# Reordering the last stage of an attention and two-layer MLP kernel: earlier operand taking, later square, separate PSUM pools

## The chip, the cores and the metric

The kernel runs on one core of a Trainium2 chip. The metric is the device time of one execution in microseconds (us), lower is better. A profiled execution gives the span of the core's instructions and the trace.

## The reference

```python
def reference(q, k, v, w1, w2, w3, w4, g_ln):      # names shortened
    x = causal_softmax_attention(q, k, v)          # 2 x 12 heads, 448 x 64, fp32
    x = x.transpose(0, 2, 1, 3).reshape(896, 768)
    h = x @ w1; x = (h * sigmoid(h)) @ w2          # 768 -> 2048 -> 768
    h = x @ w3                                     # 768 -> 1024
    e = exp(h - max(h)); s = h * e / (sum(e) + 1e-9)
    ln = (s - mean(s)) / sqrt(var(s) + 1e-6) * g_ln
    return ln @ w4                                 # 1024 -> 768
```

## The kernel before

All matrix products of the MLPs are made with operands split into a high and a low part (`fp32r`), three matmuls for each block of 128 x 128: high by high, high by low, low by high. Attention and the first MLP come first; the change touches only what follows, the second MLP.

There the 896 tokens are seven tiles of 128 (tile 0 to 6). `gemm3(t)` makes the 1024 columns of `h` of a tile in two PSUM banks. `chain(t)` makes the softmax-weighted value and its normalisation from them: VectorE (DVE) takes the negated maximum, ScalarE (ACT) the exponential, DVE the product `e * h / sum`, ACT the square with the mean as bias (written over `h` in PSUM, summed to the variance) and the shift by the mean (Identity, in place), then DVE and GpSimd (POOL) make the factor `rstd[t]`.

The last product needs `e` transposed. `turn(t)` does that on TensorE (PE), 16 small transposes into a two-bank PSUM tile `tp`. `take(t, n)` brings half n of it to SBUF: ACT copies the high part (L694), DVE makes the low part by a subtraction (L695). Tiles 0, 1 and 2 go through `whole(t, n)`: for each half n of the output two "products" of twelve matmuls each, into one of two PSUM banks (`gm`), then an ACT copy scaled by `rstd` (L739) and a store. Tiles 3 and 4, and then 5 and 6, go through `pair4`, a Strassen-like scheme with seven products for each pair, which needs sums of operand halves (made in `pre`, additions L701 on DVE, splits on ACT and POOL) and sums of weight quarters (`sums4`: four ACT scalings L833 and four POOL subtractions L835 to L838; `split_t`: four ACT copies L843 and four DVE subtractions L844). `pair4` takes its banks in turn from `psq` and `gm`.

There are 12 products in `whole` and 14 in `pair4`. After each of them `after()` runs the next entry of the table `steps`, in which the preparing work is put by hand; entry n runs behind product number n, counted from 0. Each engine works through its instructions in the order in which the program issues them. Two engines that read the same PSUM bank take turns in program order: the tile library adds a wait between them. `turn` uses the pools in the list `turns` in rotation: `pst`, and `pstb` after it has been appended. Before the change `pst` alone serves tiles 0 and 1, and `pstb` and `psq` take over the four banks of `psh`, in which `gemm3` wrote, once `chain(6)` is through.

Of the kernel before, what the change touches and what calls it, by code (L numbers as in the profile page):

```python
# [8 lines left out]
F32 = mybir.dt.float32  # L9
F32R = mybir.dt.float32r  # L10
U32 = mybir.dt.uint32
AF = mybir.ActivationFunctionType
ALU = mybir.AluOpType
# [13 lines left out]
K2 = KF2 // 2  # L27
NT = T // 128
# [52 lines left out]
def fused(ctx, tc, qk, vv, w1, w2, w3, w4, gl, out):  # L81
    nc = tc.nc
    PS = bass.MemoryType.PSUM

    def pool(name, bufs=1, **kw):
        return tc.alloc_tile_pool(name=name, bufs=bufs, **kw)
# [29 lines left out]
    with tc.manual_schedule():  # L116
# [338 lines left out]
        for step in ORDER.split():  # L455
            step, _, n = step.partition("/")
            e = {"A": nc.scalar, "V": nc.vector, "G": nc.gpsimd}.get(step[-1])
            step, _, part = step.rstrip("AVG").partition(".")
            name = step.rstrip("0123456789")
# [19 lines left out]
        for f in range(KF):  # L479
            if f == 1:  # L480
                gps[f, 1] = gm.tile([128, 512], F32, name="ps", tag="gm")
            else:
                t = pair()
# [3 lines left out]
            for half in range(2):  # L487
# [3 lines left out]
                m = 2 * f + half + 4  # L491
# [89 lines left out]
        dp = pool("dp", 1)  # L581
        pad(dp, 256)
        aop = {}
# [46 lines left out]
        hps, rstd, es4 = {}, {}, {}  # L630
        psd.release()
        pst = pool("pst", 1, space=PS)
        psh = pool("psh", 2, space=PS)

        def columns(t):
            n, b = divmod(t - 1, B)
# [1 line left out]
            return slice(o, o + 128)  # L638

        def gemm3(t):  # L640
            ps = psh.tile([128, 2, 512], F32, name="h", tag="h")
            at = columns(t)
            for n in range(2):
                for k in range(KD):
                    o = (n * KD + k) * 512
                    wh, wl = woven(w3h[:, o:o + 512]), woven(w3l[:, o:o + 512])
                    nc.tensor.matmul(ps[:, n], yh[:, k, at], wh, start=k == 0, stop=False)  # L647
                    nc.tensor.matmul(ps[:, n], yh[:, k, at], wl, start=False, stop=False)  # L648
                    nc.tensor.matmul(ps[:, n], yl[:, k, at], wh, start=False, stop=k == KD - 1)  # L649
            hps[t] = ps  # L650

        def half(t, n):
            return es4[t][:, K2 * n:K2 * n + K2]

        def chain(t, fill, fill2):
            ps = hps[t]
            s = dp.tile([128, 12], F32, name="s", tag="s", bufs=NT)
            es4[t] = dp.tile([128, KF2, 128], F32, name="e", tag="e", bufs=NT - 1)
            e, p3 = es4[t], ps.rearrange("p n (m q) -> p (n m) q", m=K2)
            col = lambda m: s[:, m:m + 1]  # L660
            nc.vector.tensor_reduce(col(0), ps, AX.XY, ALU.max, negate=True)
            nc.scalar.activation(e, p3, AF.Exp, bias=col(0), accum_out=col(1))
            fill()
            nc.vector.tensor_scalar(col(2), col(1), 1e-9, None, ALU.add)
            nc.vector.reciprocal(col(3), col(2))
            nc.vector.scalar_tensor_tensor(e, e, col(3), p3, ALU.mult, ALU.mult, accum_out=col(4))
            nc.vector.tensor_scalar(col(5), col(4), -1.0 / DF2, None, ALU.mult)
            fill2()
            nc.scalar.activation(p3, e, AF.Square, bias=col(5), accum_out=col(6))
            nc.scalar.activation(e, e, AF.Identity, bias=col(5))  # L670
            nc.vector.tensor_scalar(col(7), col(6), 1.0 / DF2, 1e-6, ALU.mult, ALU.add)
            nc.gpsimd.tensor_tensor(col(9), col(7), mhalf, ALU.pow)
            rstd[t] = col(9)

        tps = {}
# [3 lines left out]
        def rows(a):  # L679
            return a.rearrange("p k (z q) -> p k z q", q=C)  # L680

        def turn(t):
            turns.append(turns.pop(0))
            tp = turns[-1].tile([128, 2, 512], F32, name="tp", tag="tp")
            for m in range(KF2):
                for z in range(2):
                    r = slice(C * z, C * z + C)
                    nc.tensor.transpose(tp[:, z, C * m:C * m + C], es4[t][r, m], ident[r, r])
            both = tp.rearrange("p z (m q) -> p m z q", q=C)
            tps[t, 1], tps[t, 2] = both[:, :K2], both[:, K2:]  # L690

        def parts(z, x, low):
            h, l = [rows(a) for a in aop[z]]
            nc.scalar.activation(h, x, AF.Copy)  # L694
            low.tensor_tensor(l, x, h.bitcast(F32), ALU.subtract)  # L695

        def take(t, n, z=None):
            parts(z or (t, n), tps[t, n], nc.vector)

        def add(o, a, b, op):  # L700
            nc.vector.tensor_tensor(o, a, b, op)  # L701

        banks = [gm, gm]
# [28 lines left out]
        def whole(t, n):  # L732
            if n == 0:
                outs[t] = four()
            o, ps = outs[t][n], bank()
            for k in (1, 2):
                product(ps, (t, k), f"{k}{n + 1}", k == 1, k == 2)
                if k == 2:
                    nc.scalar.activation(o, ps, AF.Copy, scale=rstd[t])  # L739
                    store(t, n, o)  # L740
                after()
# [51 lines left out]
        for t in range(NT):  # L793
            gemm3(t)
            if t == 0:
                fill()
            if t == NT - 2:
                turn(0)

            def first():  # L800
                if t == NT - 2:
                    take(0, 1)
                    take(0, 2)
                fill()

            if t < NT - 1:
                chain(t, first, fill)
        area = act.tile([128, 2 * KD * T], F32R, name="area", tag="a")[:, 8:]
        places = {(1, 1): 0, (1, 2): 1, (2, 1): 2, (2, 2): 3}
        for g, at in ((1, (4, 5, 6, 7, 8, 9, None)), (2, (0, 1, 2, 3, None, 4, 5))):  # L810
# [6 lines left out]

        def arrive(t):
            turn(t)
            take(t, 1)  # L820
            take(t, 2)

        while pend:
            fill()
        w3p.release()
# [5 lines left out]
        def sums4(k):  # L831
            for n, z in enumerate(QUADS):
                nc.scalar.activation(quads[z, k], quads[z, k], AF.Copy, scale=gain[:, k + K2 * (n // 2):k + K2 * (n // 2) + 1])  # L833
            b11, b12, b21, b22 = [quads[z, k] for z in QUADS]
            nc.gpsimd.tensor_tensor(b11, b12, b11, ALU.subtract)  # L835
            nc.gpsimd.tensor_tensor(b12, b12, b22, ALU.subtract)
            nc.gpsimd.tensor_tensor(b22, b22, b11, ALU.subtract)
            nc.gpsimd.tensor_tensor(b21, b21, b22, ALU.subtract)  # L838

        def split_t(k):  # L840
            for z, q in (("t2", "22"), ("t3", "12"), ("t1", "11"), ("t4", "21")):
                h, l = split[4, z]
                nc.scalar.activation(h[:, k], quads[q, k], AF.Copy)  # L843
                nc.vector.tensor_tensor(l[:, k], quads[q, k], h[:, k].bitcast(F32), ALU.subtract)  # L844

        def pre(g, n):
            a, b = 2 * g + 1, 2 * g + 2
            s1, s3, s2, s4 = [rows(half(*at)) for at in ((b, 1), (b, 0), (a, 0), (a, 1))]
            if n == 0:
                turn(b)  # L850
                nc.scalar.activation(s3, tps[b, 1], AF.Copy)
                add(s1, tps[b, 2], s3, ALU.add)
                take(b, 2, (g, "22"))
            elif n == 1:
                turn(a)
                take(a, 1, (g, "11"))
                add(s2, s1, tps[a, 1], ALU.subtract)
                add(s3, s3, tps[a, 1], ALU.subtract)
            elif n == 2:
                take(a, 2, (g, "12"))  # L860
                add(s4, tps[a, 2], s2, ALU.subtract)
                parts((g, "s4"), s4, nc.gpsimd)
            else:
                z = ("s2", "s3", "s1")[n - 3]
                parts((g, z), {"s1": s1, "s2": s2, "s3": s3}[z], nc.gpsimd)

        steps = {1: [lambda: sums4(1)], 2: [lambda: split_t(0)], 3: [lambda: arrive(2)], 4: [lambda: sums4(2)],
                 5: [lambda: pre(1, 0)], 6: [lambda: sums4(3)], 7: [lambda: pre(1, 1)], 8: [lambda: split_t(1)],
                 9: [lambda: pre(1, 2)], 10: [lambda: split_t(2)], 11: [lambda: split_t(3), lambda: pre(1, 3)],
                 12: [lambda: pre(1, 4)], 13: [lambda: pre(1, 5)],  # L870
                 14: [lambda: pre(2, 0)], 15: [lambda: pre(2, 1)], 16: [lambda: pre(2, 2)],
                 17: [lambda: pre(2, 3), lambda: pre(2, 4)], 18: [lambda: pre(2, 5)]}
        at = iter(range(26))
# [2 lines left out]
            for step in steps.get(next(at), ()):  # L876
                step()

        def takes():
            take(1, 1)  # L880
            take(1, 2)

        sums4(0)
        turn(1)
        chain(NT - 1, takes, lambda: whole(0, 0))
        psh.release()
        psq = pool("psq", 2, space=PS)
        turns.append(pool("pstb", 1, space=PS))
        whole(0, 1)
        for t in (1, 2):  # L890
            for n in range(2):
                whole(t, n)
        banks[0] = psq
        for g in (1, 2):
            pair4(g)
        turns.remove(pst)
# [57 lines left out]
```

## Time and profile before

| | us |
|---|---|
| time, median of 3 runs | 408.81 |
| lowest and highest of them | 407.88, 411.54 |
| the profiled execution | 408.6 |
| its span | 406.8 |
| PE busy, share of the span | 396.9, 98% |
| DVE, ACT, POOL busy | 346.9, 239.7, 204.5 |

The profiled execution lies 0.2 us under the median of the runs, and its time is 1.8 us longer than its span. In the rows below a timeline line gives the start in us, the duration in us, the engine, the line of the kernel, the operation and the tiles written and read; square brackets give the idle time of the engine just before it and what ended it.

### The profile page before, as it was taken

To read this page: it belongs to the slowest core of one execution; us is meant where nothing else is said; L and a number is where in the kernel's file an instruction comes from. 1 tells how busy PE (TensorE), PEld (TensorE's weight loads), DVE (VectorE), ACT (ScalarE), POOL (GpSimd) and SP (SyncE) were. 2 spreads that over 40 slices of the span, in tenths; PEclk is the share of its full clock that TensorE was granted. 3 is DMA by queue.
4 is the path that set the end of the run, shared out by engine and by line. 5 is a ranking of instruction groups with operands and counts; after the bars stand their busy time and mean duration, and the time that the engine had idled before them with its cause. 6 is when DMAs were issued, how large, how long until landed. Compare 5 with 4: busy or idle time off the path is not lost.

```text
span 406.8 us, 7567 instructions
## 1 busy us (share of the span) xinstructions
PE 396.9 (98%) x2649; PEld 368.0 (90%) x2649; DVE 346.9 (85%) x739; ACT 239.7 (59%) x551; POOL 204.5 (50%) x222
## 2 busy tenths in 40 slices
PE   7999999999999999999999999999999999999896
PEld 5777778899999999999999999999988888889796
DVE  4999999899999999997998979867999997546843
ACT  5999999444535353534644445444658775987630
POOL 2997863377777777776453434333400010665440
PEclk9999999999999999999999999999999999999999
DMA  7775412133525242424766757555033310011121
GB/s 254 255 273 169 138 45 79 40 117 117 153 82 148 85 151 83 147 88 139 243 197 172 230 176 214 182 158 155 2 93 103 116 39 2 19 41 39 40 79 60
DMA packets 19799, 50.05 MB, mean 123 GB/s; under 512 B 2352, under 2 KB 4528, under 8 KB 19760
## 3 DMA queue, kind: packets, MB, share of 16 engines
q1 hardware_dynamic: 19760, 49.56, 39.4%
q8 instruction: 21, 0.34, 0.3%
q14 instruction: 18, 0.15, 0.1%
HBM read 46.80 MB, written 2.75 MB: 122 GB/s over the span
## 4 chain that ended last, share of the span: by engine, by line
PE 82%; DVE 8%; ACT 6%; DMA 2%; POOL 0%; SPq 0%; issue 0%; DVEq 0%
PE h L381 8%; PE h L380 8%; PE h L382 8%; PE h L510 7%; PE h L509 7%; PE h L508 7%; PE x L258 5%; PE h L647 4%; PE h L649 4%; PE h L648 4%; PE x L232 3%; DVE e L198 2%; PE x L168 2%; PE ps L715 2%; PE ps L713 2%; PE ps L714 2%
## 5 line engine op out<-in xcount | busy, mean ns | idle before, releaser
L316 POOL TENSOR_TENSOR wl<-wx,wh 128x384 fp32r<-128x384 f32 x64 | 80.6, 1261 | 73.6 <-ACT wh L312 49.0
L285 ACT ACTIVATE wr<-wr 128x384 f32<-128x384 f32 x96 | 56.7, 593 | 34.1 <-DMA wr<-w_in 34.0
L296 DVE SCALAR_TENSOR_TENSOR wx<-wr,wx 128x384 uint32<-128x384 uint32 x96 | 70.0, 730 | 0.1
L312 ACT ACTIVATE wh<-wx 128x384 fp32r<-128x384 f32 x64 | 33.1, 519 | 58.1 <-DVE wx L296 32.8
L306 DVE TENSOR_SCALAR wr<-wr 128x384 uint32<-128x384 uint32 x96 | 59.0, 614 | 3.5 <-DMA wr<-w_in 3.2
L290 DVE SCALAR_TENSOR_TENSOR wx<-wr 128x384 uint32<-128x384 uint32 x96 | 60.6, 632 | 1.3 <-POOL gl L391 1.3
L382 PE MATMUL h<-x,wl 128*128 128x448 f32 x174 | 61.3, 352 | 0.0
L380 PE MATMUL h<-x,wh 128*128 128x448 f32 x174 | 61.3, 352 | 0.0
L381 PE MATMUL h<-x,wh 128*128 128x448 f32 x174 | 61.3, 352 | 0.0
L509 PE MATMUL h<-gl,wh 128*128 128x448 f32 x160 | 56.4, 352 | 0.0
L510 PE MATMUL h<-gh,wl 128*128 128x448 f32 x160 | 56.4, 352 | 0.0
L508 PE MATMUL h<-gh,wh 128*128 128x448 f32 x160 | 56.4, 352 | 0.0
L218 POOL TENSOR_TENSOR e<-e,st 128x128 f32<-128x128 f32 (+3 forms) x70 | 44.0, 664 | 19.5 <-DVE st L211 14.7
L391 POOL TENSOR_TENSOR gl<-sg,gh 128x448 fp32r<-128x448 f32 x32 | 40.5, 1267 | 16.6 <-DVE gh L390 9.6
L204 ACT ACTIVATE e<-e,st 128x128 f32<-128x128 f32 (+3 forms) x84 | 43.6, 527 | 3.5 <-DVE st L198 3.4
L198 DVE CUSTOM_DVE_ANT_0 e<-x,mask 128x128 f32<-128x128 f32 (+3 forms) x84 | 33.1, 445 | 4.7 <-PE x L168 4.6
L382 PEld LDWEIGHTS h<-x,wl 128*128 128x128 f32 x174 | 32.9, 189 | 0.1
L381 PEld LDWEIGHTS h<-x,wh 128*128 128x128 f32 x174 | 32.9, 189 | 0.0
L380 PEld LDWEIGHTS h<-x,wh 128*128 128x128 f32 x174 | 32.9, 189 | 0.0
L647 PE MATMUL h<-w3h,y 128*128 128x512 f32 x84 | 31.9, 380 | 0.0
L648 PE MATMUL h<-w3l,y 128*128 128x512 f32 x84 | 31.8, 379 | 0.0
L649 PE MATMUL h<-w3h,y 128*128 128x512 f32 x84 | 31.8, 379 | 0.0
(204 smaller groups left out, 864.9 us busy)
## 6 DMA issues: line engine op xcount, KB each, us to landing
wr<-w_in SPq DMA_DIRECT2D x96, 384.0 KB, 3.6
qk<-qk_in SPq DMA_DIRECT2D x11, 480.0 KB, 5.4
v<-vv_in SPq DMA_DIRECT2D x12, 256.0 KB, 5.2
out<-o SPq DMA_DIRECT2D x12, 192.0 KB, 1.9
out<-o SPq DMA_DIRECT2D x4, 96.0 KB, 2.2
qk<-qk_in SPq DMA_DIRECT2D x2, 128.0 KB, 2.4
qk<-qk_in SPq DMA_DIRECT2D x1, 224.0 KB, 2.7
gain<-gl_in SPq DMA_DIRECT2D x1, 4.0 KB, 3.5
```

Of the source, the lines that this page charges most:

```text
L285: nc.scalar.activation(high, high, AF.Copy, scale=DOWN)
L290: nc.vector.scalar_tensor_tensor(x.bitcast(U32), r[:, :, 1], 0x80000000, r[:, :, 0], ALU.bitwise_and, ALU.bitwise_or)
L296: nc.vector.scalar_tensor_tensor(xu, r[:, :, 1], 3, xu, ALU.logical_shift_left, ALU.bitwise_or)
L306: nc.vector.tensor_scalar(low, low, 29, None, ALU.logical_shift_right)
L316: eng.tensor_tensor(l, wx.pop((n, c)), h.bitcast(F32), ALU.subtract)
L380: nc.tensor.matmul(ps[:, :S], wh, rh, start=turn == 0 and k % NB == 0, stop=False)
L381: nc.tensor.matmul(ps[:, :S], wh, rl, start=False, stop=False)
L382: nc.tensor.matmul(ps[:, :S], wl, rh, start=False, stop=turn == 1 and k % NB == NB - 1)
L508: nc.tensor.matmul(ps[:, :S], wh, rh, start=f == 0, stop=False)
L509: nc.tensor.matmul(ps[:, :S], wh, rl, start=False, stop=False)
L510: nc.tensor.matmul(ps[:, :S], wl, rh, start=False, stop=f == KF - 1)
L647: nc.tensor.matmul(ps[:, n], yh[:, k, at], wh, start=k == 0, stop=False)
```

## The change

- `turn(1)` and the taking of tile 1 move ahead of the last weight splits and of `sums4(0)`. They stood behind these, and the taking stood inside `chain(6)`, behind its exponential.
- `take` issues both ACT copies first and then both DVE subtractions, for all tiles. In `pre` the copies of a tile are likewise issued together, ahead of additions and subtractions.
- `chain` ends after the mean. Square, shift and `rstd` are the new function `scaled(t)`. For tiles 0 to 5 it is called straight away; for tile 6 it stands in entry 8 of `steps`, ahead of `split_t(1)`. It stood behind product 1.
- In `steps`, taking tile 2 (entry 3) and `split_t(0)` (entry 2) change places, and in entry 11 `pre(1, 3)` goes ahead of `split_t(3)`.
- `psh` becomes two pools of one tile, `psh0` on the right and `psh1` on the left. `pstb` takes the place of `psh1` before `chain(6)`, `psq` that of `psh0` after the six `whole` calls.

```diff
-        psh = pool("psh", 2, space=PS)
+        psh = [pool("psh0", 1, space=PS, side="right"), pool("psh1", 1, space=PS)]
...
-            ps = psh.tile([128, 2, 512], F32, name="h", tag="h")
+            ps = psh[t % 2].tile([128, 2, 512], F32, name="h", tag="h")
...
             fill2()
+
+        def scaled(t):
+            e, p3 = es4[t], hps[t].rearrange("p n (m q) -> p (n m) q", m=K2)
+            col = lambda m: marks[t][:, m:m + 1]
             nc.scalar.activation(p3, e, AF.Square, bias=col(5), accum_out=col(6))
             nc.scalar.activation(e, e, AF.Identity, bias=col(5))
...
+        def high(z, x):
+            nc.scalar.activation(rows(aop[z][0]), x, AF.Copy)
+
+        def low(z, x, eng):
             h, l = [rows(a) for a in aop[z]]
-            nc.scalar.activation(h, x, AF.Copy)
-            low.tensor_tensor(l, x, h.bitcast(F32), ALU.subtract)
-
-        def take(t, n, z=None):
-            parts(z or (t, n), tps[t, n], nc.vector)
+            eng.tensor_tensor(l, x, h.bitcast(F32), ALU.subtract)
+
+        def take(t):
+            for n in (1, 2):
+                high((t, n), tps[t, n])
+            for n in (1, 2):
+                low((t, n), tps[t, n], nc.vector)
...
+        arrive(1)
         while pend:
             fill()
...
             if n == 0:
                 turn(b)
                 nc.scalar.activation(s3, tps[b, 1], AF.Copy)
+                high((g, "22"), tps[b, 2])
                 add(s1, tps[b, 2], s3, ALU.add)
-                take(b, 2, (g, "22"))
+                low((g, "22"), tps[b, 2], nc.vector)
             elif n == 1:
                 turn(a)
-                take(a, 1, (g, "11"))
+                high((g, "11"), tps[a, 1])
+                high((g, "12"), tps[a, 2])
+                low((g, "11"), tps[a, 1], nc.vector)
...
-        steps = {1: [lambda: sums4(1)], 2: [lambda: split_t(0)], 3: [lambda: arrive(2)], 4: [lambda: sums4(2)],
-                 5: [lambda: pre(1, 0)], 6: [lambda: sums4(3)], 7: [lambda: pre(1, 1)], 8: [lambda: split_t(1)],
-                 9: [lambda: pre(1, 2)], 10: [lambda: split_t(2)], 11: [lambda: split_t(3), lambda: pre(1, 3)],
+        steps = {1: [lambda: sums4(1)], 2: [lambda: arrive(2)], 3: [lambda: split_t(0)], 4: [lambda: sums4(2)],
+                 5: [lambda: pre(1, 0)], 6: [lambda: sums4(3)], 7: [lambda: pre(1, 1)],
+                 8: [lambda: scaled(NT - 1), lambda: split_t(1)], 9: [lambda: pre(1, 2)], 10: [lambda: split_t(2)],
+                 11: [lambda: pre(1, 3), lambda: split_t(3)], 12: [lambda: pre(1, 4)], 13: [lambda: pre(1, 5)],
...
         sums4(0)
-        turn(1)
-        chain(NT - 1, takes, lambda: whole(0, 0))
-        psh.release()
-        psq = pool("psq", 2, space=PS)
+        psh.pop().release()
         turns.append(pool("pstb", 1, space=PS))
+        chain(NT - 1, lambda: None, lambda: whole(0, 0))
         whole(0, 1)
         for t in (1, 2):
             for n in range(2):
                 whole(t, n)
-        banks[0] = psq
+        psh.pop().release()
+        psq = banks[0] = pool("psq", 2, space=PS, side="right")
```

## Rows read from the trace of the kernel before

**Rows 1.** Page, part 2: the granted clock in 40 slices of the span.
```profile
PEclk9999999999999999999999999999999999999999
```

**Rows 2.** Timeline of PE, last stage: its beginning, a regular `turn`, its end.
```profile
343.22 0.38 PE L649 MATMUL h<-w3h,y 128*128 128x512 f32 x1
...
363.29 0.33 PE L715 MATMUL ps<-b22h,area 128*128 128x384 f32 x1
363.55 0.71 PE L688 MATMUL tp<-ident,e 64*128 64x64 f32 x16
364.19 0.43 PE L713 MATMUL ps<-b11h,area 128*128 128x384 f32 x1
364.46 0.33 PE L714 MATMUL ps<-b11l,area 128*128 128x384 f32 x1
...
400.98 0.33 PE L713 MATMUL ps<-t4h,area 128*128 128x384 f32 x1
...
402.77 0.33 PE L715 MATMUL ps<-t4h,area 128*128 128x384 f32 x1
```

**Rows 3.** Timeline of PE: its four waits behind 343 us.
```profile
353.19 0.71 PE L688 MATMUL tp<-ident,e 64*128 64x64 f32 x16 [0.96 <-DVE s L664]
...
359.45 0.43 PE L713 MATMUL ps<-b12h,area 128*128 128x384 f32 x1 [0.80 <-ACT o L739]
...
378.96 0.43 PE L713 MATMUL ps<-t2h,area 128*128 128x384 f32 x1 [0.20 <-ACT area L694]
...
380.86 0.43 PE L715 MATMUL ps<-t2h,area 128*128 128x384 f32 x1 [1.31 <-POOL area L695]
```

**Rows 4.** Timeline of ACT, 346 to 359 us.
```profile
346.27 1.10 ACT L600 ACTIVATE b22h<-wx,gain 128x384 fp32r<-128x384 f32 x2
347.28 2.12 ACT L833 ACTIVATE wx<-wx,gain 128x384 f32<-128x384 f32 x4
349.30 1.09 ACT L662 ACTIVATE e<-h,s 128x1024 f32<-128x1024 f32 x1
...
351.73 0.60 ACT L694 ACTIVATE area<-tp 128x512 fp32r<-128x512 f32 x1 [0.76 <-DVE area L695]
352.22 0.57 ACT L739 ACTIVATE o<-ps,s 128x384 f32<-128x384 f32 x1
...
354.85 1.12 ACT L669 ACTIVATE h<-e,s 128x1024 f32<-128x1024 f32 x1
...
357.18 0.51 ACT L843 ACTIVATE t2h<-wx 128x384 fp32r<-128x384 f32 x1
...
358.84 0.56 ACT L739 ACTIVATE o<-ps,s 128x384 f32<-128x384 f32 x1
```

**Rows 5.** Timeline of DVE, 346 to 374 us.
```profile
346.90 1.15 DVE L605 SCALAR_TENSOR_TENSOR b22l<-wx,gain,b22h 128x384 fp32r<-128x384 f32 x2 [1.26 <-ACT b22h L600]
347.96 1.22 DVE L661 TENSOR_REDUCE s<-h 128x1 f32<-128x1024 f32 x1
...
368.57 0.69 DVE L695 TENSOR_TENSOR area<-tp,area 128x512 fp32r<-128x512 f32 x1 [2.27 <-ACT area L694]
369.18 1.27 DVE L701 TENSOR_TENSOR e<-e,tp 128x512 f32<-128x512 f32 x2
370.37 0.97 DVE L844 TENSOR_TENSOR t2l<-wx,t2h 128x384 fp32r<-128x384 f32 x1
371.27 0.55 DVE L844 TENSOR_TENSOR t3l<-wx,t3h 128x384 fp32r<-128x384 f32 x1
```

**Rows 6.** Timeline of POOL, 369 to 379 us.
```profile
369.92 1.01 POOL L838 TENSOR_TENSOR wx<-wx 128x384 f32<-128x384 f32 x1
374.69 1.28 POOL L695 TENSOR_TENSOR area<-e,area 128x512 fp32r<-128x512 f32 x1 [3.76 <-ACT area L694]
```

**Rows 7.** Instructions of line 316, 282 to 285.5 us: duration least/median/most, starts.
```profile
L316 POOL TENSOR_TENSOR w3l<-wx,w3h x3: 1005/1047/1093, 282.6 to 285.1; 128x384 fp32r<-128x384 f32 x3
L316 DVE TENSOR_TENSOR w3l<-wx,w3h x3: 1055/1353/1365, 283.0 to 285.2; 128x384 fp32r<-128x384 f32 x3
```

More of the change, by code (lines that the diff above doesn't have):

```diff
@@ L653, in half @@
             return es4[t][:, K2 * n:K2 * n + K2]
+        marks = {}
         def chain(t, fill, fill2):
             ps = hps[t]
-            s = dp.tile([128, 12], F32, name="s", tag="s", bufs=NT)
+            s = marks[t] = dp.tile([128, 12], F32, name="s", tag="s", bufs=NT)
             es4[t] = dp.tile([128, KF2, 128], F32, name="e", tag="e", bufs=NT - 1)
@@ L690, in turn @@
             tps[t, 1], tps[t, 2] = both[:, :K2], both[:, K2:]
-        def parts(z, x, low):
+        def high(z, x):
+            nc.scalar.activation(rows(aop[z][0]), x, AF.Copy)
+        def low(z, x, eng):
             h, l = [rows(a) for a in aop[z]]
-            nc.scalar.activation(h, x, AF.Copy)
-            low.tensor_tensor(l, x, h.bitcast(F32), ALU.subtract)
-        def take(t, n, z=None):
-            parts(z or (t, n), tps[t, n], nc.vector)
+            eng.tensor_tensor(l, x, h.bitcast(F32), ALU.subtract)
[4 more added lines that the diff above has]
+                low((t, n), tps[t, n], nc.vector)
         def add(o, a, b, op):
@@ L801, in first @@
                 if t == NT - 2:
-                    take(0, 1)
-                    take(0, 2)
+                    take(0)
                 fill()
@@ L807, in fused @@
                 chain(t, first, fill)
+                scaled(t)
         area = act.tile([128, 2 * KD * T], F32R, name="area", tag="a")[:, 8:]
@@ L819, in arrive @@
             turn(t)
-            take(t, 1)
-            take(t, 2)
+            take(t)
+        arrive(1)
         while pend:
@@ L859, in pre @@
             elif n == 2:
-                take(a, 2, (g, "12"))
+                low((g, "12"), tps[a, 2], nc.vector)
                 add(s4, tps[a, 2], s2, ALU.subtract)
-                parts((g, "s4"), s4, nc.gpsimd)
+                high((g, "s4"), s4)
+                low((g, "s4"), s4, nc.gpsimd)
             else:
                 z = ("s2", "s3", "s1")[n - 3]
-                parts((g, z), {"s1": s1, "s2": s2, "s3": s3}[z], nc.gpsimd)
-        steps = {1: [lambda: sums4(1)], 2: [lambda: split_t(0)], 3: [lambda: arrive(2)], 4: [lambda: sums4(2)],
-                 5: [lambda: pre(1, 0)], 6: [lambda: sums4(3)], 7: [lambda: pre(1, 1)], 8: [lambda: split_t(1)],
-                 9: [lambda: pre(1, 2)], 10: [lambda: split_t(2)], 11: [lambda: split_t(3), lambda: pre(1, 3)],
-                 12: [lambda: pre(1, 4)], 13: [lambda: pre(1, 5)],
+                x = {"s1": s1, "s2": s2, "s3": s3}[z]
+                high((g, z), x)
+                low((g, z), x, nc.gpsimd)
+        steps = {1: [lambda: sums4(1)], 2: [lambda: arrive(2)], 3: [lambda: split_t(0)], 4: [lambda: sums4(2)],
+                 5: [lambda: pre(1, 0)], 6: [lambda: sums4(3)], 7: [lambda: pre(1, 1)],
+                 8: [lambda: scaled(NT - 1), lambda: split_t(1)], 9: [lambda: pre(1, 2)], 10: [lambda: split_t(2)],
+                 11: [lambda: pre(1, 3), lambda: split_t(3)], 12: [lambda: pre(1, 4)], 13: [lambda: pre(1, 5)],
                  14: [lambda: pre(2, 0)], 15: [lambda: pre(2, 1)], 16: [lambda: pre(2, 2)],
@@ L877, in after @@
                 step()
-        def takes():
-            take(1, 1)
-            take(1, 2)
         sums4(0)
-        turn(1)
-        chain(NT - 1, takes, lambda: whole(0, 0))
-        psh.release()
-        psq = pool("psq", 2, space=PS)
+        psh.pop().release()
         turns.append(pool("pstb", 1, space=PS))
+        chain(NT - 1, lambda: None, lambda: whole(0, 0))
         whole(0, 1)
```

## The prediction

> **What bounds the kernel now.** I read the page first: PE is busy in 98% of the span (the table above) and its granted clock is at the full level in all 40 slices [rows 1], so only time in which PE stands still can be won, and the price of a matmul stays as it is. Next the waits of PE behind 325 us, where the changed code starts, and PE's timeline there: four waits, 0.96 + 0.80 + 0.20 + 1.31 = 3.27 us of idle time [rows 3]. The reader is to see what each of them waits for.
>
> - At 353.19 the turn of tile 2 wants `tp` free, from which DVE still makes tile 1's second low part; the row names the DVE instruction behind it. Tile 1 is late because its two ACT copies stand behind the exponential of tile 6 at 349.30, and ACT then sat idle for 0.76 us ahead of the second copy, at 351.73, until DVE's first subtraction was through, though the two share no data [rows 4].
> - At 359.45 the second half of tile 1 wants its bank, and the ACT copy that empties it ran only at 358.84, behind Square and Identity of tile 6 (from 354.85) and four weight copies (from 357.18) [rows 4].
> - At 378.96 and 380.86 the product with `s2` wants first the high part from ACT, then the low part from POOL; the high part stands behind `split_t(3)` in entry 11 of `steps`, and the low part waits for it.
>
> **What PE's time would be without waits.** A matmul of this stage steps by (402.77 - 400.98) / 11 = 0.163 us, so a product of twelve takes 1.95 us. A regular turn puts 364.46 - 363.29 = 1.17 us where two steps would be 0.33, so it costs 0.845 us [rows 2]. From the last matmul of `gemm3` to the last of all, 343.22 to 402.77, pass 59.55 us. The stage has 26 products and 6 turns: 26 x 1.95 + 6 x 0.845 = 55.77 us. The difference, 3.78 us, is the four waits with the refill of PE behind each. The change alters neither number, so **3.78 us is the most that it can win**; what stands in front of 343 us has no PE wait behind 325, and the 4.0 us from the last matmul to the end of the span stay.
>
> **The change part by part.** I walk the new queues with the durations of the old rows and ask at each place when PE wants the result. I leave PE without waits: it is done with `gemm3` at 343.38, so product number n (from 1) starts at 343.38 + 1.95 (n - 1) + 0.845 for each turn ahead of it.
>
> Tile 1 at once. ACT is free for it at 346.27, where the last weight splits began [rows 4]. I take that start unchanged, though taking tile 0 in the new order should let it come some tenths earlier. Two copies at 0.49 (351.73 to 352.22) end at 347.36. DVE's subtractions read the same tile, and the 0.76 us row shows that reads of it by two engines take turns in program order, so the first goes behind both copies: 347.40, then 0.61 each (368.57 to 369.18), the second ending at 348.70. The turn of tile 2 now stands behind product 3 and is asked for at 343.38 + 5.85 + 0.845 + 0.1 = 350.2. **The first wait goes, with 1.5 us to spare.**
>
> What this pushes back: on ACT the weight splits (1.01) and `sums4(0)` (2.02) end at 350.28 instead of 349.30. On DVE the two weight subtractions (1.06) now start at 348.62 and the maximum of tile 6 (1.22) ends at 350.90 instead of 349.18 [rows 5]. The exponential goes from 350.92 to 352.01, and the copy that empties the first bank, queued behind it, ends at 352.58. Product 5 wants this bank at 343.38 + 7.80 + 2 x 0.845 = 352.87. **Only 0.29 us to spare, the tightest place**; every tenth by which this chain is later than that costs a tenth.
>
> Square and shift out of the way. The copy of the second bank now follows `sums4(1)` (2.02) and tile 2's two copies (0.98): 352.58 + 3.00 = 355.58, done at 356.15. Product 7 wants the bank at 343.38 + 11.70 + 3 x 0.845 = 357.62. **The second wait goes, with 1.5 us to spare.**
>
> Where they come instead. From 356.15 ACT does `split_t(0)` (358.84 - 357.18 = 1.66), `sums4(2)` 2.02, a bank copy 0.57, two copies of tile 4 0.98, `sums4(3)` 2.02, a bank copy 0.57, two copies of tile 3 0.98, and is at 364.95. Square and Identity take 357.18 - 354.85 = 2.33 us [rows 4], to 367.28; `split_t(1)` starts there. Queued behind them is the chain that feeds `s4`: four weight subtractions on DVE at 0.55, from the end of the first copy (0.51) at 367.8 to 370.0, tile 3's second subtraction (0.61) and an addition (0.64), to 371.3 [rows 5], then ACT's high part (0.60, as for a copy of a tile) and POOL's low part (1.28 [rows 6]), done at 373.2. The third matmul of product 15 wants it at 343.38 + 27.30 + 3.38 + 0.33 = 374.4: **1.2 us to spare**, after the 2.33 that were put in here. The other followers of tile 6 have room: its turn wants Identity's result at 376.0, nearly nine us later, and product 13 wants the bank that Square writes at 370.2, four us behind Square. No DMA is moved past another; the stores keep their order on SP.
>
> `pre(1, 3)` ahead of `split_t(3)`. The high part of `s2` follows that of `s4`, `split_t(2)` and a bank copy: 371.9 + 1.66 + 0.57 = 374.1, done at 374.7; POOL's low part is done at 376.0. Product 16 wants the high part at 376.9, the low part at 377.2. **Both last waits go, with 1.2 us and more to spare**; the weight parts now behind it are wanted for the last quarter of that product, at 378.3, and DVE has the first of them near 376.5.
>
> Pools that stand apart cost nothing: `psh1` was last read by tile 5's Square before 346.3, and the turn that takes its place comes at 356.8.
>
> One cost has no row for the new place. POOL's 16 subtractions (1.01 us each [rows 6]) now run beside `split_t(0)`, whose DVE subtractions start near 356.9. A DVE subtraction that met one took 0.97 us instead of 0.55 [rows 5, 6]. Line 316 shows both engines at it together: POOL starts three in 2.5 us, DVE three in 2.2, that is, they take turns at some 1.24 us [rows 7]. By the lower bound, 0.55 a piece, nothing is late; by turns, 1.24, the four end at 361.9 and an addition and a subtraction of tile 4 behind them by 363.2, ahead of tile 3's copies: nothing either. I take the second, as its rows show the same pair of engines and operations; it costs PE no time. The Trainium skill, page "SBUF — State Buffer", section "Who interferes with whom", has the rule behind this: a VectorE instruction with two SBUF inputs and a GpSimd one that reads SBUF exclude each other, and the second to issue blocks until the first is finished. The trace agrees with the 0.97 us above; who is served in a run of both the rule leaves to the order of issue, and with strict turns the sum stays as it is.
>
> **The sum.** 0 left of 3.78: the profiled execution of 408.60 would become 404.8. It lies 0.2 us under the median of the runs, so by that it is 405.0. I forecast **405.0 us**. The likeliest case's own range is 404.2 to 405.6.
>
> **The rivals.**
>
> - A part of the waits stays. For it speak the 0.29 us at product 5 and the 1.2 us behind Square, both worked out over a dozen steps. A DVE queue 1 us later costs 0.7 at product 5, an `s4` chain 2 us later 0.8; with one or both, 405.7 to 406.5. Against it: tile 0's new order gives the first chain something back, and the second is reckoned with full durations where the queues step faster.
> - Port to POOL in part. If POOL keeps its turn as long as it has work, DVE's first weight subtractions get in only in the hole between POOL's second and third group of four, of under a microsecond near 358, and the fourth goes behind the last group, which ends near 367. All of DVE's queue comes behind: 0.55 + 1.25 + 3 x 0.62 + 0.2 + 4 x 0.55 + 0.61 bring tile 3's second subtraction to 373.7, 1.3 us after product 14 wants it at 372.4, and the steps behind it (0.64 + 0.60 + 1.28) add 0.5 at product 15 and about as much at 16. Some 2.4 us: 407.3. Against it: rows 7 show turns.
> - **Slower**: the same without the hole, which closes when the third group's scalings come a microsecond sooner. Then all four subtractions stand behind 367, 3 x 0.55 = 1.65 us more, 4.05 in all: 409.0. It decides from the point where POOL's third group starts before the first of these subtractions has run. For it speaks only that DVE waited 0.4 us at 370.37, against it rows 7.
> - The change doesn't do what it says: the wait of the turn at 350.2 stays, as `tp` is still read. That needs tile 1's copies 1.5 us later than ACT is free. Then 1.0 comes back: 406.0.
>
> **How the numbers follow.** Forecast 0.72, a part stays (the unmoved turn included) 0.17, port in part 0.06, slower 0.05. The lowest run shown lies 0.9 us under the median; with that and the first three cases the range goes from 403.9 to 407.3, and what it leaves out above is the slower case and a disturbed median. A measurement of this kernel can tell about 1%, 4.1 us, from no change. The full gain of 3.78 is 0.92%, just under it, so scatter decides: of the forecast's 0.72 I give 0.30 to faster by over 1% and the rest to within 1%. Both middle rivals lie within 1%; of the slower case's 0.05, at 409.0, only a worse form would pass 1%, so 0.03: 0.30, 0.67, 0.03.
>
> **What would show it.** Right: no PE wait behind 343 us over 0.1 us, the last matmul near 399.0, 26 products at 1.95; ACT's second copy of a tile straight behind the first; Square of tile 6 near 364. Wrong: a PE wait on ACT's `o` copy near 353, on an `area` part of POOL near 374 or 377 us, or DVE's line of weight subtractions standing still for several POOL instructions in a row from 357 on.

## The result, and the profile after

| | before | after |
|---|---|---|
| median, us (8 runs each) | 409.40 | 405.28 |
| lowest to highest | 407.88 to 411.54 | 404.75 to 406.13 |
| profiled execution, its span | 408.6, 406.8 | 405.16, 403.4 |

The ratio after to before is 0.9899, 95% interval 0.9873 to 0.9925. In a later comparison on another occasion the same kernel came to 0.9905 (0.9883 to 0.9927). The forecast was 405.0 us, a gain of 3.78 us or 0.92%, and this lies in both intervals.

The profiles compare best by **the last stage**, from the start of the last matmul of `gemm3` to the start of the last matmul of all. What lies ahead of it scatters: that matmul starts between 343.14 and 344.57 us in the profiles of this document, the two of before and after included. The list of PE's waits behind 320 us is empty after the change. The timeline of PE after, the rows that answer to [rows 2, 3]:

```profile
343.54 0.38 PE L649 MATMUL h<-w3h,y 128*128 128x512 f32 x1
...
350.54 0.71 PE L694 MATMUL tp<-ident,e 64*128 64x64 f32 x16
...
353.24 0.33 PE L724 MATMUL ps<-b11h,area 128*128 128x384 f32 x1
...
357.87 0.43 PE L724 MATMUL ps<-b12h,area 128*128 128x384 f32 x1
...
377.10 0.43 PE L724 MATMUL ps<-t2h,area 128*128 128x384 f32 x1
377.37 0.33 PE L725 MATMUL ps<-t2l,area 128*128 128x384 f32 x1
377.53 0.33 PE L726 MATMUL ps<-t2h,area 128*128 128x384 f32 x1
...
399.33 0.33 PE L726 MATMUL ps<-t4h,area 128*128 128x384 f32 x1
```

None of the four places where PE stood still has a bracket any more. The stage is 399.33 - 343.54 = 55.79 us, against 59.55 before and 55.77 worked out. Of the 3.76 us won the profiled pair shows 3.4, as the stage began 0.32 us later in the second.

What ACT does now, against [rows 4]:

```profile
346.24 1.07 ACT L699 ACTIVATE area<-tp 128x512 fp32r<-128x512 f32 x2
347.20 1.12 ACT L600 ACTIVATE b22h<-wx,gain 128x384 fp32r<-128x384 f32 x2
348.21 2.12 ACT L844 ACTIVATE wx<-wx,gain 128x384 f32<-128x384 f32 x4
350.86 1.11 ACT L664 ACTIVATE e<-h,s 128x1024 f32<-128x1024 f32 x1 [0.52 <-DVE s L663]
...
351.96 0.58 ACT L750 ACTIVATE o<-ps,s 128x384 f32<-128x384 f32 x1
...
355.41 0.58 ACT L750 ACTIVATE o<-ps,s 128x384 f32<-128x384 f32 x1
...
364.41 1.15 ACT L675 ACTIVATE h<-e,s 128x1024 f32<-128x1024 f32 x1
...
370.71 0.63 ACT L699 ACTIVATE area<-e 128x512 fp32r<-128x512 f32 x1 [1.72 <-DVE e L712]
...
373.36 0.63 ACT L699 ACTIVATE area<-e 128x512 fp32r<-128x512 f32 x1
```

The two copies of tile 1 (346.24) run back to back. The first bank is emptied at 351.96 + 0.58 = 352.54, and product 5 wants it at 353.24: 0.7 us of room. The second is empty at 355.99 and wanted at 357.87. Square of tile 6 runs at 364.41.

DVE and POOL at the place without a row before, `split_t(0)` beside `sums4`, first DVE, then POOL:

```profile
356.76 0.61 DVE L855 TENSOR_TENSOR t2l<-wx,t2h 128x384 fp32r<-128x384 f32 x1
357.29 1.36 DVE L855 TENSOR_TENSOR t3l<-wx,t3h 128x384 fp32r<-128x384 f32 x1
358.57 0.55 DVE L855 TENSOR_TENSOR t1l<-wx,t1h 128x384 fp32r<-128x384 f32 x1
359.04 1.36 DVE L855 TENSOR_TENSOR t4l<-wx,t4h 128x384 fp32r<-128x384 f32 x1
```

```profile
357.03 1.20 POOL L849 TENSOR_TENSOR wx<-wx 128x384 f32<-128x384 f32 x1
358.72 1.26 POOL L846 TENSOR_TENSOR wx<-wx 128x384 f32<-128x384 f32 x1 [0.49 <-ACT wx L844]
360.06 1.20 POOL L847 TENSOR_TENSOR wx<-wx 128x384 f32<-128x384 f32 x1
```

A DVE subtraction that meets one of POOL's takes 1.36 us and lets it pass, one in POOL's pause takes 0.55; POOL's take 1.2 instead of 1.0. The four are through at 360.4.

### The profile page after: what moved, and what is told of

It reads as the page before. It is cut to its first block, busy times and chain, and to the rows that moved or that the text cites. A ratio compares the mean times of both kernels' runs of the same rounds, so it can differ in the third digit from the quotient of the medians.

```text
span 403.4 us, 7574 instructions
## 1 busy us (share of the span) xinstructions
PE 396.8 (98%) x2649; PEld 368.2 (91%) x2649; DVE 347.5 (86%) x739; ACT 238.8 (59%) x551; POOL 206.6 (51%) x222
## 4 chain that ended last, share of the span: by engine, by line
PE 94%; DVE 4%; ACT 0%; issue 0%; DVEq 0%; SPq 0%
PE h L382 8%; PE h L381 8%; PE h L380 8%; PE h L508 8%; PE h L510 8%; PE h L509 7%; PE x L258 5%; PE h L647 5%; PE h L649 4%; PE h L648 4%; PE ps L724 4%; PE ps L726 4%; PE ps L725 4%; PE x L168 3%; PE x L232 3%; DVE e L198 3%
## 5 line engine op out<-in xcount | busy, mean ns | idle before, releaser
L316 POOL TENSOR_TENSOR wl<-wx,wh 128x384 fp32r<-128x384 f32 x64 | 81.8, 1280 | 72.4 <-ACT wh L312 50.1
L312 ACT ACTIVATE wh<-wx 128x384 fp32r<-128x384 f32 x64 | 33.1, 519 | 58.5 <-DVE wx L296 39.5
```

The source lines that it names most:

```text
L316: eng.tensor_tensor(l, wx.pop((n, c)), h.bitcast(F32), ALU.subtract)
```

## The experiments

The theory is the prediction's: each engine's queue is shared, so a wait taken from PE is won only if the next result on the same queues is in time, and the edits hold each other up. The main rival says that each of the four waits belongs to one edit, and the gains add up. The stage length of the profile is the measure. Two profiles of the changed kernel give 55.79 and 55.80 us; the kernel before has one profile only. The times are single ones except where a median is named.

| kernel | stage, us | time, us |
|---|---|---|
| before | 59.55 | 408.6 |
| after; after again (e11) | 55.79; 55.80 | 405.16; 404.94 (median of 6) |
| e1 tile 1 at once, alone | 59.85 | 409.32 (median of 10) |
| e2 taking in the old order | 56.23 | 405.91 |
| e3 `split_t(3)` first | 56.04 | 405.61 |
| e4 square back | 56.36 | 405.63 |
| e5 one more maximum | 56.46 | 406.18 |
| e6 `sums4(2)` sooner | 55.79 | 405.61 |
| e7 tile 1 back | 58.13 | 408.03 |
| e8 the two large moves alone | 59.61 | 409.13 (median of 10) |
| e9 turns of 128 x 128 | 56.01 | 405.65 (median of 6) |
| e10 the same, taking in the old order | 56.24 | 406.21 |

**e1: tile 1 at once, in the kernel before.**

```diff
+        arrive(1)
         while pend:
             fill()
...
         sums4(0)
-        turn(1)
-        chain(NT - 1, takes, lambda: whole(0, 0))
+        chain(NT - 1, lambda: None, lambda: whole(0, 0))
```

> The kernel before, with one edit: tile 1 is turned and taken ahead of the last weight splits. Measured by the last stage, from the start of the last matmul of gemm3 to the start of the last matmul: 59.55 us before, 55.79 after. Theory of shared queues (a wait that is taken away is handed to the next thing that is late on the same queue): the wait of 1.0 at the turn of tile 2 goes, but PE then comes 1.0 sooner to the bank copy that still stands behind Square and Identity and waits 1.7 there instead of 0.8, with small new waits at the copies behind it; the two waits at the s2 product stay. Stage 59.2 to 59.7, time as before. Rival (each wait belongs to one edit and they add up): stage 58.5, 1.0 us faster.

The time is 1.0008 of before (0.9988 to 1.0027): nothing won. PE's waits in the stage (who waited for whom: us in all, how often, the longest):

```profile
PE ps L713 <- ACT o L739: 1.8, 2, 1.6
PE ps L715 <- POOL area L695: 1.3, 1, 1.3
PE ps L713 <- ACT area L694: 0.2, 1, 0.2
```

The wait of the turn, 0.96 in [rows 3], is off the list, and the wait for the bank copy grew from 0.80 to 1.63 with a second of 0.16 behind it. What was taken from the first wait came back in full at the bank copies. The stage is even 0.3 longer, a little over the 59.2 to 59.7 that I expected: the short wait costs PE 0.43 us, as the recorded duration of the matmul ahead covers 0.17 of it and the step behind it takes 0.27 instead of 0.16 us (the refill). The rival's 58.5 is out.

**e7: the reverse, the changed kernel with tile 1 back.**

```diff
-        arrive(1)
         while pend:
             fill()
...
         psh.pop().release()
+        turn(1)
         turns.append(pool("pstb", 1, space=PS))
-        chain(NT - 1, lambda: None, lambda: whole(0, 0))
+        chain(NT - 1, lambda: take(1), lambda: whole(0, 0))
```

> The changed kernel, with tile 1 turned behind sums4(0) and taken behind the exponential of tile 6, as before the change. Theory of shared queues: the turn of tile 2, which the change put one product earlier, waits for it some 2.4 us; everything behind has that much more room. Stage 58.0 to 58.4. Rival (each wait belongs to one edit): the old wait of 1.0 comes back, stage 56.8.

```profile
353.42 0.71 PE L694 MATMUL tp<-ident,e 64*128 64x64 f32 x16 [2.28 <-DVE s L666]
```

One wait of 2.28 us at the turn of tile 2, more than the 0.96 before, because the change asks for this turn one product earlier. The same edit is worth nothing in the one kernel and 2.3 us in the other.

**e8: the two large moves without the rest.**

```diff
         def take(t):
             for n in (1, 2):
                 high((t, n), tps[t, n])
-            for n in (1, 2):
                 low((t, n), tps[t, n], nc.vector)
...
-        steps = {1: [lambda: sums4(1)], 2: [lambda: arrive(2)], 3: [lambda: split_t(0)], 4: [lambda: sums4(2)],
+        steps = {1: [lambda: sums4(1)], 2: [lambda: split_t(0)], 3: [lambda: arrive(2)], 4: [lambda: sums4(2)],
...
-                 11: [lambda: pre(1, 3), lambda: split_t(3)], 12: [lambda: pre(1, 4)], 13: [lambda: pre(1, 5)],
+                 11: [lambda: split_t(3), lambda: pre(1, 3)], 12: [lambda: pre(1, 4)], 13: [lambda: pre(1, 5)],
```

In `pre`, too, the order is as before; e2 below shows that part of the edit.

> The changed kernel with only its two largest moves left: tile 1 at once, and the late square and shift of tile 6. The order of taking, tile 2's place (entry 3 behind split_t(0)) and entry 11 are as before the change. Theory of shared queues: ACT's idle time at each taking and the weight copies ahead of the bank copies bring the waits back in other places, at products 9 and 11 and at the products with s4 and s2; stage 58.5 to 60, little or nothing gained on the kernel before. Rival (these two moves are the change, the rest is trimming): stage 55.8 to 57.

Ratio 1.0010 (0.9987 to 1.0033), stage 59.61: the whole gain is gone, though both moves of the title are in. The row on ACT from which it works without a pause to the bank copy that product 9 waits for (362.88):

```profile
360.36 0.60 ACT L699 ACTIVATE area<-tp 128x512 fp32r<-128x512 f32 x1 [2.97 <-DVE area L703]
```

Tile 2's second copy stands behind its first subtraction on DVE, that behind `split_t(0)`'s subtractions, and those meet POOL's. ACT loses 3 us there, and PE waits 0.95 and 0.16 at bank copies, 0.35 for `s4`, 0.40 and 0.82 for `s2`. The three smaller edits together are what keeps ACT from waiting for DVE there. Two of them were also taken back alone (e2 and e3 below, 0.44 and 0.25 us); the exchange of entries 2 and 3 was not, so its own share is not shown.

**e2: only the taking as before.** The same edit of `take`, and in `pre`:

```diff
                 nc.scalar.activation(s3, tps[b, 1], AF.Copy)
-                high((g, "22"), tps[b, 2])
                 add(s1, tps[b, 2], s3, ALU.add)
+                high((g, "22"), tps[b, 2])
                 low((g, "22"), tps[b, 2], nc.vector)
...
                 high((g, "11"), tps[a, 1])
-                high((g, "12"), tps[a, 2])
                 low((g, "11"), tps[a, 1], nc.vector)
...
+                high((g, "12"), tps[a, 2])
                 low((g, "12"), tps[a, 2], nc.vector)
```

> The changed kernel, with the order of taking as before: each ACT copy followed by its DVE subtraction, in take and in pre. Theory of shared queues: ACT stands idle some 0.8 us at each of the takings of tile 2, 4 and 3, which makes Square of tile 6, the weight splits behind it and the first weight part of the s2 product late: a PE wait of 0.5 to 1.0 us at the product with s2, stage 56.3 to 56.8. Rival (the idle time of ACT lies off the path, as the other edits leave over a microsecond of room): stage 55.8 to 55.9.

Stage 56.23, 0.44 longer, a little under what the theory gave and far over the rival. The list of PE's waits is empty, and yet PE lost the time; it stands on the weight loads (PEld):

```profile
PEld ps L725 <- POOL area L703: 0.4, 2, 0.2
```

Two loads, at the products with `s2` and `s3`, waited 0.20 us each for POOL's low part. The recorded duration of the matmul ahead covers that in PE's row; with the refill behind it each costs some 0.18 us, 0.36 of the 0.44, and 0.08 stands at the second matmul of product 5. So the wait at the product with `s2` is there, but smaller than the 0.5 to 1.0 us expected.

**e3: entry 11 as before.**

```diff
-                 11: [lambda: pre(1, 3), lambda: split_t(3)], 12: [lambda: pre(1, 4)], 13: [lambda: pre(1, 5)],
+                 11: [lambda: split_t(3), lambda: pre(1, 3)], 12: [lambda: pre(1, 4)], 13: [lambda: pre(1, 5)],
```

> The changed kernel, with split_t(3) ahead of pre(1, 3) in entry 11, as before the change. Theory of shared queues: the s2 parts come 1.66 us later, which their room of over a microsecond and the time since won on ACT nearly cover; stage 55.8 to 56.3. Rival (this edit is what took away the two waits at the s2 product, 0.26 and 1.47): they come back, stage 57.3.

```profile
377.88 0.19 PEld L726 LDWEIGHTS ps<-t2h,area 128*128 128x128 f32 x1 [0.28 <-POOL area L703]
```

0.25 us, by one weight load that waited 0.28 us for POOL. So this edit does not own the two old waits of 0.20 and 1.31: most of them went because ACT comes to this place sooner even without it. The high part of `s2` starts 375.30 - 343.75 = 31.55 us into the stage here, against 378.29 - 343.22 = 35.07 before.

**e4: square and shift back behind product 2.**

```diff
         chain(NT - 1, lambda: None, lambda: whole(0, 0))
+        scaled(NT - 1)
...
-                 8: [lambda: scaled(NT - 1), lambda: split_t(1)], 9: [lambda: pre(1, 2)], 10: [lambda: split_t(2)],
+                 8: [lambda: split_t(1)], 9: [lambda: pre(1, 2)], 10: [lambda: split_t(2)],
```

> The changed kernel, with square and shift of tile 6 back behind the first two products, ahead of tile 2's taking. Theory of shared queues: ACT's 2.3 us come ahead of the copy of the second bank, which has 1.5 to 1.8 us of room: a PE wait of 0.5 to 0.9 us at product 7, and at most 0.3 later; stage 56.3 to 56.8. Rival (with tile 1 taken early the queue has room for them wherever they stand): stage 55.8.

```profile
358.31 0.43 PE L724 MATMUL ps<-b12h,area 128*128 128x384 f32 x1 [0.50 <-ACT o L750]
```

A wait of 0.50 at product 7 and nothing later: 2.3 us of ACT work ahead of a copy with 1.9 us of room.

**e5: one more maximum on the tightest chain.**

```diff
         sums4(0)
+        again = dp.tile([128, 1], F32, name="again", tag="again", bufs=1)
+        nc.vector.tensor_reduce(again, hps[NT - 1], AX.XY, ALU.max, negate=True)
         psh.pop().release()
```

> The changed kernel, with one more DVE maximum of tile 6's 1024 columns (1.15 us a step, its result unused) ahead of the real one. It lies on the chain that I called the tightest: maximum, exponential, copy of the first bank, product 5. Theory (0.29 us of room by the old rows, 0.6 by the rows of the changed kernel): a PE wait of 0.5 to 0.9 at product 5 and nothing later, stage 56.3 to 56.7. Rival (the chain has room, something else bounds PE): 55.8. Rival (no room): 57.0.

```profile
354.16 0.43 PE L724 MATMUL ps<-b11h,area 128*128 128x384 f32 x1 [0.40 <-ACT o L750]
```

The stage grew by 0.67 us for 1.15 us of DVE work, by one wait at product 5: 0.40 in the bracket, 0.17 that the duration of the matmul ahead covers (0.33 for a step of 0.16), and 0.1 of refill. So the chain was 0.57 late and had some 0.6 us of room, between the 0.29 worked out ahead and the 0.7 read off the rows after, and it is the tightest of the places read here.

**e6: POOL without a hole.**

```diff
-        steps = {1: [lambda: sums4(1)], 2: [lambda: arrive(2)], 3: [lambda: split_t(0)], 4: [lambda: sums4(2)],
+        steps = {1: [lambda: sums4(1)], 2: [lambda: arrive(2)], 3: [lambda: sums4(2), lambda: split_t(0)],
```

> The changed kernel, with sums4(2) moved from entry 4 to entry 3, ahead of split_t(0): POOL gets its third group of subtractions early enough to work on without a hole, while DVE asks for its first weight subtractions in the middle of it. Theory (POOL and DVE take turns): each of these four DVE subtractions ends 1.2 to 1.4 us behind the one before, they are through by about 363, PE waits nowhere, stage 55.8. Rival (POOL keeps the port while it has work): DVE's subtractions stand until POOL's last one of the sums, near 367, PE waits for tile 3's second half and for s4 and s2, 3 us in all or more, stage 58.8 or more.

DVE's and POOL's timeline:

```profile
358.97 0.96 DVE L855 TENSOR_TENSOR t2l<-wx,t2h 128x384 fp32r<-128x384 f32 x1 [1.60 <-ACT t2h L854]
359.86 1.36 DVE L855 TENSOR_TENSOR t3l<-wx,t3h 128x384 fp32r<-128x384 f32 x1
361.14 1.36 DVE L855 TENSOR_TENSOR t1l<-wx,t1h 128x384 fp32r<-128x384 f32 x1
362.42 1.36 DVE L855 TENSOR_TENSOR t4l<-wx,t4h 128x384 fp32r<-128x384 f32 x1
```

```profile
358.50 1.02 POOL L846 TENSOR_TENSOR wx<-wx 128x384 f32<-128x384 f32 x1
359.60 1.20 POOL L847 TENSOR_TENSOR wx<-wx 128x384 f32<-128x384 f32 x1
360.88 1.21 POOL L848 TENSOR_TENSOR wx<-wx 128x384 f32<-128x384 f32 x1
362.16 1.20 POOL L849 TENSOR_TENSOR wx<-wx 128x384 f32<-128x384 f32 x1
363.33 1.32 POOL L846 TENSOR_TENSOR wx<-wx 128x384 f32<-128x384 f32 x1
```

POOL works without a pause and DVE gets one subtraction in after each of POOL's, 1.28 us apart. The stage is 55.79, unchanged. The rival that gave the slower case, POOL keeping the port, is refuted at the very condition it named. The Trainium skill, page "SBUF — State Buffer", section "Who interferes with whom", states that a VectorE instruction with two SBUF inputs contends with a GpSimd one that reads SBUF. The trace agrees, with 1.36 us beside POOL for 0.55 alone; who is next in a run of both is shown by these rows alone.

**e9 and e10: the turn itself.** With PE never waiting, the turns are what is left beside the products.

```diff
-            for m in range(KF2):
-                for z in range(2):
-                    r = slice(C * z, C * z + C)
-                    nc.tensor.transpose(tp[:, z, C * m:C * m + C], es4[t][r, m], ident[r, r])
-            both = tp.rearrange("p z (m q) -> p m z q", q=C)
-            tps[t, 1], tps[t, 2] = both[:, :K2], both[:, K2:]
+            for m in range(KF2):
+                o = 2 * C * (m % K2)
+                nc.tensor.transpose(tp[:, m // K2, o:o + 2 * C], es4[t][:, m], ident)
+            both = tp.rearrange("p n (m z q) -> p n m z q", z=2, q=C)
+            tps[t, 1], tps[t, 2] = both[:, 0], both[:, 1]
```

> The changed kernel, with each turn made of 8 transposes of 128 x 128 instead of 16 of 64 rows, the first half of the tile in one PSUM bank and the second half in the other (before, each half lay in both banks). With no PE wait left, the six regular turns at 0.845 us are what the stage has beside its products; their 16 transposes step by 0.04 us. Theory: PE is bound, so what a turn loses in length the stage loses, six times. If a transpose goes by its columns at the matmuls' 0.42 ns a column, 8 of them take 0.43 instead of 0.64 us: stage 54.5 instead of 55.79, some 1.3 us faster than the changed kernel. Rival (a transpose of fp32 costs more a column than these products, and the 64-row ones ran beside each other): 0.85 us and more a turn, stage 57 or longer. As a side effect ACT's copy of one half should no longer stand in DVE's way at the other half: DVE's first subtraction of a tile starts behind the first copy.

> The same with the old order of taking, each ACT copy followed by its DVE subtraction. Theory (ACT's idle time of 0.76 us at each taking came from two engines' reads of one PSUM bank taking turns): with the halves in banks of their own it is gone, the second copy follows the first straight away though DVE's subtraction is issued between them, and the stage is as long as with the new order. Rival (the wait has another cause, such as the tile or the buffers written): ACT still stands 0.7 us ahead of each second copy and the stage is some 0.4 us longer.

> The changed kernel once more, on the same chip as the two others, to compare with: stage 55.8, 405 us.

e9, PE's timeline at a turn, against the regular turn in [rows 2]:

```profile
351.35 0.33 PE L725 MATMUL ps<-b12h,d 128*128 128x384 f32 x1
351.52 1.04 PE L693 MATMUL tp<-ident,e 128*128 128x128 f32 x8
352.31 0.41 PE L723 MATMUL ps<-b22h,d 128*128 128x384 f32 x1
352.55 0.33 PE L724 MATMUL ps<-b22l,d 128*128 128x384 f32 x1
```

Eight transposes take 0.79 us to the next product, 0.099 each, where sixteen of half the rows take 0.64. The gap ahead is shorter (0.17 for 0.26 us), so a turn comes to 1.20 us instead of 1.17, and six of them to the 0.2 us that the stage grew. My estimate by columns, 0.43 us a turn, was wrong and the rival right in sign, though its 57 us or longer was out too. The side effect that I expected did not come either: DVE's first subtraction of tile 1 starts at 348.38, behind both of ACT's copies (347.28 to 348.34), though the half that it reads lies in a bank of its own. The time is 0.9913 of before (0.9887 to 0.9938), not to be told from the changed kernel's 0.9905 on the same chip.

e10 went against me too. ACT's row at tile 1:

```profile
348.46 0.60 ACT L698 ACTIVATE area<-tp 128x512 fp32r<-128x512 f32 x1 [0.76 <-DVE area L702]
```

With the halves in banks of their own the second copy still waits 0.76 us for DVE's subtraction of the first, and the stage is 0.23 us longer than in e9 (the rival said 0.4). So the wait does not go by the bank alone, as the description of the kernel before has it. The two instructions share the tiles `tp` and `area`. That it is not `area` shows in two places. ACT writes to `area` at 377.99 in the profile after, while POOL's subtractions into it, which the program issues earlier, run until 379.88. And at tile 4 of e10 ACT's copy goes to `d` and DVE's addition ahead of it to `e`, so that only `tp` is left in common:

```profile
363.39 0.60 ACT L698 ACTIVATE d<-tp 128x512 fp32r<-128x512 f32 x1 [0.76 <-DVE e L710]
```

That leaves the tile `tp` as a whole; no run changes that alone. For the change this makes no difference: the order of issue decides, and two copies issued together have no such wait between them.

No variant beat the changed kernel. Two parts of the change have no run of their own: the exchange of entries 2 and 3, and the two pools. The late square needs the pools apart, as it still writes to `psh0` after `pstb` has taken the place of `psh1`; that they cost nothing rests on the empty list of waits.

## Why the prediction was right

- **The most that can be won.** 26 products and 6 turns gave 55.77 us; the profile after shows 55.79 with no wait. That one number carried the forecast: a stage whose bound engine has neither more nor fewer instructions can only lose its waits. The 405.0 itself had some luck: it started from a median of three runs, 408.81, and eight runs gave 409.40, from which 3.78 less is 405.6.
- **Tile 1 at once.** The first wait went. The room was there: DVE is through with tile 1 at 347.34 + 1.29 = 348.63 and the turn starts at 350.54, straight behind product 3, 1.9 us later (1.5 predicted).
- **The tightest place.** 0.29 us worked out, 0.7 by the rows after, 0.6 by the test of e5. Most of the difference is the gain on tile 0's taking, which I had named and left out: ACT is free for tile 1 at 346.24 - 343.54 = 2.70 us into the stage, against 346.27 - 343.22 = 3.05 before. e2, with the old order alone, has 346.91 - 343.85 = 3.06 again.
- **Square and shift.** Predicted "near 364", measured 364.41. The second bank, whose copy used to stand behind them, has 1.9 us of room (355.99 to 357.87; 1.5 predicted). In their new place the chain to `s4` ends in time: its high part starts at 370.71, POOL's low part ends at 371.42 + 1.29 = 372.71, and product 15 starts at 374.42.
- **The `s2` product.** I gave the gain to `pre(1, 3)` going ahead of `split_t(3)` and found 1.2 us of room with it. e3 shows that 0.25 us at most hangs on that order. The gain came from the whole queue being earlier. The sum held; this attribution was too narrow.
- **POOL and DVE.** They take turns, 1.28 us a step in e6 for the 1.24 taken from line 316. Both forms of the port rival are out.
- **What I did not see.** I walked the change as a whole and so never met that the two large moves alone win nothing (e8) and the first alone nothing either (e1). The order of taking, which I counted only as a few tenths at tile 0, is worth 0.44 us alone (e2) and, with the places in `steps`, the whole gain (e8).

The measured 4.1 us by the medians and 3.76 us by the stage agree within the interval. Whether it passes 1% the runs don't settle: 0.9899 and 0.9905.

## What to carry to other kernels

Where one engine has to issue a fixed list of instructions, count what that list takes and compare: the difference is all that reordering can give, and it is also a test of the result. Then follow every other queue through the new order and note the room at each hand-over, because a wait removed alone can come back in full, as in e1, at the next late result on the same queue. Issue the reads of one engine from a shared tile together, so that two engines don't wait for each other in the middle of a tile.

## What the runs showed of the hardware

- A wait of 0.2 to 0.3 us on PE's weight loads can be missing from PE's own list (e2, e3), as the recorded 0.33 us of the matmul ahead lasts 0.17 us beyond its step.
- DVE and POOL, both with all inputs in SBUF, alternate one by one when both have work (e6): 1.36 us recorded for a DVE subtraction of 0.55, 1.20 for POOL's of 1.01, a step of 1.28.
- A transpose of 128 x 128 fp32 steps by 0.099 us, one of 64 rows by 0.040: for the same tile 0.79 against 0.64 us.
